# Attention scores, AV and a feed-forward layer on one core: AV fills its third PSUM tile last, and the exponentials of the second half are read in another order

## The chip, the cores and the metric

The kernel runs on one core of a Trainium2 chip. The core has a matmul engine (TensorE, "PE" in the profile; its weight loads stand as "PEld"), three engines for elementwise work (VectorE "DVE", ScalarE "ACT", GpSimd "POOL"), SyncE ("SP"), which here only issues transfers, and transfers between memory and the chip (DMA). The engines run side by side, each through its own queue in order, and wait for one another by semaphores. PE writes its results to PSUM; only ACT and DVE read them from there. The metric is the device time of one execution in microseconds; a kernel's time is the median of several executions.

## The reference

Inputs are q, k and v of shape (8, 8, 576, 64) (batch, heads, positions, head size) and two weight matrices of 512 x 2048 and 2048 x 512, all float32. Two attentions are added, and a feed-forward layer follows:

```python
q_d = q.reshape(B, H, Sd, 4, D).mean(axis=3)      # also k_d, v_d; Sd = 144
out_up = np.repeat(sm_attn(q_d, k_d, v_d), 4, axis=2)
mask = np.abs(pos[:, None] - pos[None, :]) < 4    # each position sees 7
out_local = softmax(where(mask, q @ k.T / sqrt(D), -1e9)) @ v
x = (out_up + out_local) as (4608 tokens, 512)
h = x @ w_in
out = (h / (1 + exp(-1.702 * h))) @ w_out
```

"Down" below is the attention over the 144 pooled positions, "local" the banded one over all 576.

## The kernel before

The feed-forward layer runs in nine groups of 512 tokens (`n_groups`, L1056). For each group `mm1` (L869) multiplies by w_in: 16 blocks of 128 hidden features, four matmuls of 512 columns each (L854), read out by ACT with the activation function (L865). Then `mm2` (L893) multiplies by w_out: 64 matmuls (L930) into two PSUM tiles PM in turn, read out by ACT (L915) and stored by SP.

The attention of batch b = g + 1 runs inside group g. The order of all engines is written out by hand (L43 to L45); there is no planner. `attention` (L804) gives five steps, and the list `POS` (L959) says before which matmul block each is issued: positions below 16 count the blocks of `mm1`, the others the matmuls of `mm2`. For batches 2 to 7 the steps are:

- position 12: scores of the first half (heads 0 to 3) on PE (`scores_mixed`, L402);
- position 16: their exponentials on ACT (`s_act`, L815), then the masks on DVE (`mask_local`, L459);
- position 33, that is before matmul 17 of `mm2`: scores of the second half (heads 4 to 7), and their exponentials and masks;
- position 41, before matmul 25, eight matmuls later: `avx` (L691) of heads 0 to 3, the weighted sums ("AV");
- position 53, before matmul 37, twelve matmuls later: `avx` of heads 4 to 7.

Batches 0 and 1 go by other functions.

Three PSUM tiles PA[0], PA[1], PA[2], of two banks each, serve the attention. The scores of a half lie in all three: down scores in PA[0], local scores in PA[1] and PA[2]. `exp_down` (L453) reads PA[0] into `ed`; `exp_local` (L446) reads PA[1] and then PA[2] into two `es` tiles (L448), in the loop `for u in range(2)`. In the second half `exp_down` comes first, so that ACT reads PA[0], PA[1], PA[2]. `mask_local` multiplies the two `es` tiles by the band mask in the order of their numbers.

`avx` then writes its sums over the same tiles. Its matmuls are short (57 to 144 columns) and use a quarter of the array each, so that four run side by side. `down` (L697) puts the pooled attention of one pair of heads into PA[0] and of the other into PA[2], numerators and denominators in turn, six calls of four matmuls (L701). `local` (L709, its matmul at L723) has three uses: `main` and `extra` with the calls beside them go to PA[0] and PA[2] (40 matmuls), `rest` and `rest_den` to PA[1] (24 matmuls). The order before is written at L744 to L760: `rest` and `rest_den` lie between the calls of `down`, and the main part follows.

What follows reads the tiles out (L765 to L772): ACT takes logarithms of the denominators in PA[0], PA[2] and PA[1], DVE copies the numerators in the same order (L767, L771), and ACT's exponential of the negated logarithms (L772) gives the reciprocals. DVE multiplies (L777), the pooled part is added (L793) by POOL for heads 0 to 3 and by DVE for heads 4 to 7, and xT is ready for `mm1`.

For the next batch DVE transposes q and k (`prep_1`, L284), and POOL sums them over four positions (`pool_qk`, L315 and L319), casts v (L325) and sums v into `vd` (`prep_v4`, L332 and L335). `down` needs `vd`.

Of the kernel before, what the change touches and what calls it, by code (L numbers as in the profile page):

```python
# [19 lines left out]
def kernel(  # L20
# [359 lines left out]
    def scores(b, qd, barred=False, sp=None):  # L380
        sp = sp or [ps_tile(), ps_tile()]
        if barred:
            bar_others(sp)
        for i in range(5):
            for a in range(2):
                for par in range(2):
                    for r in range(4):
                        rows = slice(32 * r, 32 * r + 32)
                        k0 = 114 * i + KSTART[par]
                        q0 = 114 * i + QSTART[par]  # L390
                        nc.tensor.matmul(  # L391
                            sp[r // 2][64 * par : 64 * par + 64, r % 2, 60 * i : 60 * i + 60],
                            lhsT=kT[b, qd][rows, k0 : k0 + 64, a],
                            rhs=qT[b, qd][rows, q0 : q0 + 60, a],
                            start=(a == 0 and not barred),
                            stop=(a == 1 or barred),
                            tile_position=(32 * r, 64 * par),
                            skip_group_check=barred,
                        )
        return sp  # L400

    def scores_mixed(b, qd, P):  # L402
        def local(i, a, half):
            for r in range(4):
                par = half if r < 2 else 1 - half
                rows = slice(32 * r, 32 * r + 32)
                k0 = 114 * i + KSTART[par]
                q0 = 114 * i + QSTART[par]
                nc.tensor.matmul(  # L409
                    P[1 + r // 2][64 * par : 64 * par + 64, r % 2, 60 * i : 60 * i + 60],  # L410
                    lhsT=kT[b, qd][rows, k0 : k0 + 64, a],
                    rhs=qT[b, qd][rows, q0 : q0 + 60, a],
                    start=(a == 0), stop=(a == 1),
                    tile_position=(32 * r, 64 * par),
                )

        if qd:
            for n in range(10):
                local(n // 2, n % 2, 0)
        for n in range(6):  # L420
            scores_d(b, qd, P[0], (n,))
            for a in range(2 if n < 5 else 0):
                local(n, a, 1)
        if not qd:
            for n in range(10):
                local(n // 2, n % 2, 0)
        return P[0], P[1:3]

    def scores_d(b, qd, sd=None, rounds=range(6)):
        sd = sd or ps_tile()  # L430
        bank = banks(sd)
        for n in rounds:
            kc, a = n // 2, n % 2
            for r in range(4):
                rows = slice(32 * r, 32 * r + 32)
                u, j = (r // 2, r % 2) if b < 2 else (r % 2, r // 2)
                nc.tensor.matmul(  # L437
                    bank[u][64 * j : 64 * j + 64, SD * kc : SD * kc + SD],
                    lhsT=kdT[qd][rows, 48 * kc : 48 * kc + 64, a],
                    rhs=qdT[b, qd][rows, :, a],  # L440
                    start=(a == 0), stop=(a == 1),
                    tile_position=(32 * r, 64 * j),
                )
        return sd

    def exp_local(qd, sp):  # L446
        for u in range(2):
            nc.scalar.activation(  # L448
                out=es[2 * qd + u][:, :, 0:300], in_=sp[u][:, :, 0:300],
                func=AF.Exp, scale=inv_sqrt_d,  # L450
            )
# [12 lines left out]
    def av(b, hp, n=None):  # L464
        o = ps_tile(n)
        av_local(b, hp, o)
        av_down(b, hp, o)
        return o
# [222 lines left out]
    def avx(b, hps):  # L691
# [5 lines left out]
        def down(kc, den):  # L697
            for u, hp in enumerate(hps):
                rows = slice(64 * u, 64 * u + 48)
                for j in range(2):  # L700
                    nc.tensor.matmul(  # L701
                        mains(u)[64 * j : 64 * j + 64, den, DN : DN + SD],
                        lhsT=ones[rows, 1, :] if den else vd[rows, kc, hp // 2 * 2 + j, 0:D],
                        rhs=eds[hp // 2][rows, j, SD * kc : SD * kc + SD],
                        start=(kc == 0), stop=(kc == 2),
                        tile_position=(64 * u, 64 * j),
                    )

        def local(den, to, what):  # L709
            for par in range(2):  # L710
                hp = hps[par] if to == "main" else hps[1 - par]
                i, c0, ni, n = what[par]
                rows = slice(64 * par, 64 * par + 64)
                if to == "rest":
                    t, bk = PA[1], par
                    at = 256 * den + 57 * (i - 1 + par)
                else:
                    t, bk = mains(par), den
                    at = 57 * i + c0 if par == 0 else 57 * i
                    if to == "extra":  # L720
                        at = EX
                for j in range(2):
                    nc.tensor.matmul(  # L723
                        t[64 * j : 64 * j + 64, bk, at : at + ni * n],
                        lhsT=ones[rows, 0, :] if den else vb[rows, i, 2 * hp + j, 0:D],
                        rhs=sub(es[hp][rows, j, :], 60 * i + c0, (60, ni), (1, n)),
                        start=True, stop=True,
                        tile_position=(64 * par, 64 * j),
                    )

        def rest(k):
            local(0, "rest", ((k + 1, 3, 1, 57), (k, 0, 1, 57)))

        def rest_den(k):
            local(1, "rest", ((k + 1, 3, 2, 57), (k, 0, 2, 57)))

        def main(k):
            local(0, "main", ((k, 3 if k else 0, 1, 57 if k else 60),
                              (k, 0, 1, 57 if k < 4 else 60)))

        def extra(den):
            local(den, "extra", ((0, 0, 1, 60), (4, 0, 1, 60)))

        for kc in range(3):  # L744
            down(kc, 0)
            rest(kc)
            down(kc, 1)
            if kc < 2:
                rest_den(2 * kc)
        rest(3)  # L750
        main(0)
        local(1, "main", ((1, 3, 2, 57), (0, 0, 2, 57)))
        main(1)
# [4 lines left out]
        extra(0)  # L758
        main(4)
        extra(1)  # L760

        l = work.tile([128, 2, S + SD], FP32, name="l", tag="l", bufs=2)
        n = work.tile([128, 2, S + SD], FP32, name="n", tag="n", bufs=1)
# [40 lines left out]
    def attention(b, slots=None):  # L804
        st = {}
        exps = "exp_and_others" if b == 1 else "natural_log_exp_and_others"

        def s_pe(qd):
            if b > 1:
                st["d", qd], st["s", qd] = scores_mixed(b, qd, PA)  # L810
                return
            st["d", qd] = scores_d(b, qd, PB[0])
            st["s", qd] = scores(b, qd, sp=PB[1:3])

        def s_act(qd):  # L815
            if qd == 0:
                nc.scalar.preload_act_table_set(exps)
            if b == 1 or qd:
                exp_down(qd, st["d", qd])
            exp_local(qd, st["s", qd])  # L820
            if b > 1 and not qd:
                exp_down(qd, st["d", qd])
            if qd == 1 and b == 1:
                nc.scalar.preload_act_table_set("silu_and_others")
            mask_local(qd)

        def s1():
            s_pe(1)
            s_act(1)

        def avn(*hps):
            def f():
                for hp in hps:
                    st["o", hp] = av(b, hp, slots and slots[hp % 2])
                for hp in hps:
                    st["y", hp] = normalise(st["o", hp])
            return f

        def tr(*hps):
            def f():  # L840
                for hp in hps:
                    st["x", hp] = transp(st["y", hp], slots and slots[hp % 2])
                for hp in hps:
                    od = copy_od(st["x", hp])
                    merge(b, hp, st["x", hp], od)
            return f

        first = [lambda: s_pe(0), lambda: s_act(0), s1]
        if b == 1:
            return first + [avn(0, 1), tr(0), tr(1), avn(2, 3), tr(2), tr(3)]  # L850
        return first + [lambda: avx(b, (0, 1)), lambda: avx(b, (2, 3))]
# [141 lines left out]
    sp = scores(0, 0, barred=True, sp=PA[0:2])  # L993
# [9 lines left out]
    sp = scores(0, 1, barred=True, sp=PA[0:2])  # L1003
# [52 lines left out]
    for g in range(n_groups):  # L1056
        b = g + 1
# [69 lines left out]
```

## Time and profile before

| what | value |
|---|---|
| median of 3 runs | 320.76 us (320.55 to 321.66) |
| profiled execution | 320.15 us |
| its span | 318.4 us |
| granted TensorE clock | 1.00 |
| PE busy | 305.3 us, 96% of the span |
| ACT, POOL, DVE busy | 200.1, 158.0, 141.9 us |
| one steady group (128.05 to 160.89 us) | 32.84 us, PE busy 32.75, ACT 23.58, POOL 20.76, DVE 17.54 |

A row of the timeline gives start, length, engine, line, operation, output and inputs with the tile's shape, and the number of instructions merged; a bracket says how long the engine stood idle before and whose end let it go on. The chain that ended last is followed back from the last instruction, at each step to what released it; its rows give start, length, and the engine and line. Matmuls are pipelined: one that begins while its predecessor is under way adds to the busy time, so the distance between two starts says more about PE than the length of a row.

### The profile page before, as it was taken

The numbers are of one execution on the slowest core, as the hardware profiler recorded it, in microseconds if no ns is written. First come the engines' busy times: TensorE is split into PE (matmuls) and PEld (weight loads), VectorE is DVE, ScalarE is ACT, GpSimd is POOL, SyncE is SP. The second block draws the span as 40 slices with busy tenths as digits, with TensorE's granted clock in tenths as the row PEclk, the third lists the DMA queues.
The fourth block names the chain that finished last, engine by engine and source line by source line (L and its number), as shares of the span: only waits on it lengthen the run. The fifth ranks groups of instructions, "written<-read, shape, count | busy, mean of one in ns | idle before, by whom it ended". The sixth has DMA issues, their size and how long they took to land.

```text
span 318.4 us, 10134 instructions
## 1 busy us (share of the span) xinstructions
PE 305.3 (96%) x4434; PEld 153.8 (48%) x4434; DVE 141.9 (45%) x283; ACT 200.1 (63%) x321; POOL 158.0 (50%) x183
## 2 busy tenths in 40 slices
PE   6688999999999999999999999999999999999995
PEld 2454454445554455445545454555445544444444
DVE  6983425820597049803890379127922580000000
ACT  4474782566786678557955885687568757315611
POOL 8883960198336963497339833992398020000000
PEclk9999999999999999999999999999999999999999
DMA  6999999999616980599149924993330110020011
GB/s 119 121 190 210 186 128 209 200 227 220 142 64 171 199 167 36 162 203 197 41 143 191 180 88 128 187 191 95 115 104 1 69 71 0 18 81 35 0 66 66
DMA packets 64124, 39.98 MB, mean 126 GB/s; under 512 B 44624, under 2 KB 54992, under 8 KB 64080
## 3 DMA queue, kind: packets, MB, share of 16 engines
q0 software_dynamic: 18864, 14.95, 33.1%
q1 hardware_dynamic: 45072, 24.32, 30.1%
q8 instruction: 34, 0.56, 0.8%
q14 instruction: 10, 0.08, 0.1%
q10 hardware_dynamic: 144, 0.07, 0.1%
HBM read 44.83 MB, written 9.44 MB: 170 GB/s over the span
## 4 chain that ended last, share of the span: by engine, by line
PE 88%; ACT 6%; DMA 4%; issue 1%; POOL 1%; DVE 0%; POOLq 0%
PE pm L930 33%; PE pm L854 26%; PE pa L854 14%; PE pa L409 3%; PE pa L930 2%; DMA qb<-in_q_dram 2%; PE pa L437 2%; PE pa L701 2%; ACT es L448 2%; PE pa L723 2%; ACT ed L454 2%; DMA vb<-in_v_dram 1%; PE pm L945 1%; PE pa L391 0%; ACT L1018 0%
## 5 line engine op out<-in xcount | busy, mean ns | idle before, releaser
L930 PE MATMUL pm<-w_out_bf,gT 128*128 128x512 bf16 x528 | 119.6, 379 | 0.0
L854 PE MATMUL pm<-xT,w_in_bf 128*128 128x512 bf16 x376 | 93.9, 379 | 0.7 <-ACT gT L865 0.5
L854 PEld LDWEIGHTS <-w_in_bf 128*128 128x128 bf16 x576 | 55.7, 98 | 67.1 <-issue 1.3
L865 ACT ACTIVATE gT<-pm 128x512 bf16<-128x512 f32 x94 | 56.2, 602 | 43.6 <-PE pm L854 43.6
L930 PEld LDWEIGHTS <-gT 128*128 128x128 bf16 x560 | 52.6, 98 | 61.1 <-issue 0.2
L462 DVE TENSOR_TENSOR es<-es,mask 128x600 bf16<-128x600 bf16 x28 | 18.8, 685 | 90.2 <-ACT es L448 89.4
L854 PE MATMUL pa<-xT,w_in_bf 128*128 128x512 bf16 x200 | 53.3, 379 | 0.0
L915 ACT ACTIVATE osb<-pm 128x512 f32<-128x512 f32 (+2 forms) x35 | 20.4, 582 | 32.8 <-PE pm L930 30.1
L793 POOL TENSOR_TENSOR xT<-xT,od 128x576 bf16<-128x576 bf16 x12 | 17.7, 1471 | 41.8 <-DVE xT L777 41.3
L315 POOL TENSOR_TENSOR pq<-kT 128x576 f32<-128x576 bf16 x14 | 16.2, 1157 | 37.9 <-DVE kT L284 37.8
L865 ACT ACTIVATE gT<-pa 128x512 bf16<-128x512 f32 x50 | 29.0, 607 | 5.6 <-PE pa L854 5.6
L777 DVE TENSOR_TENSOR xT<-n,l 128x285 bf16<-128x285 f32 (+1 forms) x96 | 28.2, 368 | 0.0
L332 POOL TENSOR_TENSOR pq<-v 112x512 f32<-112x512 f32 x18 | 24.0, 1331 | 0.8 <-DMA v<-in_v_dram 0.8
L917 DVE TENSOR_SCALAR osb<-pm 128x128 f32<-128x128 f32 x1 | 0.3, 293 | 53.5 <-ACT osb L915 53.5
L448 ACT ACTIVATE es<-pa 128x600 bf16<-128x600 f32 x32 | 19.7, 669 | 1.8 <-PE pa L391 1.7
L284 DVE STREAM_TRANSPOSE kT<-kb 128x576 f32<-128x576 f32 x16 | 19.9, 1247 | 1.8 <-DMA kb<-in_k_dram 1.8
L284 DVE STREAM_TRANSPOSE qT<-qb 128x576 f32<-128x576 f32 x16 | 19.9, 1242 | 0.2 <-DMA qb<-in_q_dram 0.2
L767 DVE COPY n<-pa 128x492 f32<-128x492 f32 x24 | 15.0, 665 | 9.2 <-ACT l L766 8.2
L766 ACT ACTIVATE l<-pa 128x492 f32<-128x492 f32 x24 | 12.6, 578 | 9.9 <-PE pa L723 9.9
L454 ACT ACTIVATE ed<-pa 128x864 bf16<-128x864 f32 x16 | 14.3, 894 | 5.3 <-PE pa L437 5.3
L772 ACT ACTIVATE l<-l 128x1440 f32<-128x1440 f32 x12 | 16.8, 1404 | 0.4
L237 POOL DMA_DIRECT2D vb<-in_v_dram x20 | 13.7, 700 | 5.9 <-DMA w_in_bf<-in_moe_w_in_dram 3.4
(120 smaller groups left out, 356.8 us busy)
## 6 DMA issues: line engine op xcount, KB each, us to landing
out_dram<-osb SPq DMA_DIRECT2D x34, 256.0 KB, 2.1
vf<-in_v_dram SPq DMA_DIRECT2D x60, 128.0 KB, 5.0
v<-in_v_dram SPq DMA_DIRECT2D x72, 96.0 KB, 3.3
kb<-in_k_dram POOLq DMA_DIRECT2D x16, 288.0 KB, 6.7
qb<-in_q_dram POOLq DMA_DIRECT2D x16, 288.0 KB, 8.9
w_out_bf<-in_moe_w_out_dram POOLq DMA_DIRECT2D x4, 512.0 KB, 13.3
vb<-in_v_dram POOLq DMA_DIRECT2D x20, 64.0 KB, 5.7
w_in_bf<-in_moe_w_in_dram POOLq DMA_DIRECT2D x2, 512.0 KB, 7.6
```

Source lines behind the costliest of these rows:

```text
L284: nc.vector.transpose(out=t32.rearrange("p (i c) -> p c i", c=18), in_=store[b, qd].bitcast(FP32).rearrange("p (c d) -> p c d", c=18),)
L332: eng.tensor_tensor(out=t1[0:112], in0=x[:, :, 0:2, :], in1=x[:, :, 2:4, :], op=ALU.add)
L448: nc.scalar.activation(out=es[2 * qd + u][:, :, 0:300], in_=sp[u][:, :, 0:300], func=AF.Exp, scale=inv_sqrt_d,)
L454: nc.scalar.activation(out=eds[qd][:, :, 0:432], in_=sd[:, :, 0:432], func=AF.Exp, scale=inv_sqrt_d / 16.0,)
L462: nc.vector.tensor_tensor(out=ev, in0=ev, in1=mask, op=ALU.mult)
L772: nc.scalar.activation(out=l, in_=l, func=AF.Exp, scale=-1.0)
L777: nc.vector.tensor_tensor(out=out, in0=sub(n, *part), in1=sub(l, *part), op=ALU.mult)
L793: eng.tensor_tensor(out=xs, in0=xs, in1=sub(od[:, u, :], 0, (1, SD), (0, 4)), op=ALU.add)
L854: nc.tensor.matmul(acc, lhsT=w_in_bf[:, dmc, ffc * 128 : (ffc + 1) * 128], rhs=xT[dmc][:, g * TG : g * TG + TG], start=(dmc == 0), stop=(d ...
L865: nc.scalar.activation(out=gT[:, ffc, :], in_=acc, func=AF.Silu, scale=GELU_SCALE)
L915: eng.activation(out=osb, in_=ap, func=AF.Copy, scale=1.0 / GELU_SCALE)
L930: nc.tensor.matmul(ops[t], lhsT=gT[:, ffc, t * 128 : (t + 1) * 128], rhs=w_out_bf[:, ffc, :], start=(ffc == 0), stop=(ffc == n_ffc - 1),)
```

## The change

In `avx` the calls that fill PA[1] move behind all others: the loop keeps the six `down` calls, and `rest` and `rest_den` come after `extra(1)`, in an order of their own. `exp_local` gets a parameter for the order of its two reads, and for batches from 2 on the second half (`qd` = 1) reads PA[2] before PA[1]. What is computed stays the same, and so do the number and the shapes of all instructions. `avx` runs twice in each of the batches 2 to 7; the exponentials' new order holds for the second half of each of them.

```diff
-    def exp_local(qd, sp):
-        for u in range(2):
+    def exp_local(qd, sp, us=(0, 1)):
+        for u in us:
             nc.scalar.activation(
                 out=es[2 * qd + u][:, :, 0:300], in_=sp[u][:, :, 0:300],
                 func=AF.Exp, scale=inv_sqrt_d,
...
         for kc in range(3):
             down(kc, 0)
-            rest(kc)
             down(kc, 1)
-            if kc < 2:
-                rest_den(2 * kc)
-        rest(3)
         main(0)
         local(1, "main", ((1, 3, 2, 57), (0, 0, 2, 57)))
         main(1)
...
         extra(0)
         main(4)
         extra(1)
+        for k in range(4):
+            rest(k)
+            if k % 2 == 0:
+                rest_den(k)
...
-            exp_local(qd, st["s", qd])
+            exp_local(qd, st["s", qd], (0, 1) if b == 1 or not qd else (1, 0))
```

## The prediction

> **What bounds the kernel now.** I read the page first: engine shares and the chain that ended last. The span is 318.4 us, the profiled execution 320.15 us.
>
> ```profile
> PE 305.3 (96%) x4434; PEld 153.8 (48%) x4434; DVE 141.9 (45%) x283; ACT 200.1 (63%) x321; POOL 158.0 (50%) x183
> ...
> PE 88%; ACT 6%; DMA 4%; issue 1%; POOL 1%; DVE 0%; POOLq 0%
> ```
>
> TensorE (PE) is the bound, yet 6% of the chain lies on ACT. A busy share can't show why: a short matmul counts some 0.2 us as busy and overlaps its successors, so it covers small gaps. So I took the chain in order of time for one steady batch, batch 4.
>
> ```profile
> 147.91 0.02 issue
> 147.93 0.89 ACT ed L454
> 148.82 1.13 ACT es L448 x2
> 149.95 0.04 issue
> 150.00 0.22 PE pa L701
> ```
>
> The second half's scores end at 147.91; the chain then leaves PE for the three exponentials of the half and returns 2.09 us later, at AV's "down" matmuls (L701). Between these, PE issued only eight matmuls of the second projection: 8 x 0.216 = 1.73 us. The remaining 0.36 us is a stall, met at the last of the three exponentials. The PE timeline of batch 3 names it.
>
> ```profile
> 114.87 1.90 PE L930 MATMUL pm<-w_out_bf,gT 128*128 128x512 bf16 x8
> 116.70 0.25 PE L701 MATMUL pa<-ed,vd 48*64 48x144 bf16 x2
> 117.16 0.25 PE L701 MATMUL pa<-ed,vd 48*64 48x144 bf16 x2 [0.20 <-ACT es L448]
> ...
> 118.25 2.76 PE L930 MATMUL pm<-w_out_bf,gT 128*128 128x512 bf16 x12
> 120.94 0.26 PE L701 MATMUL pa<-ed,vd 48*64 48x144 bf16 x4
> ...
> 122.05 3.20 PE L930 MATMUL pm<-w_out_bf,gT 128*128 128x512 bf16 x14
> ```
>
> Two "down" matmuls, into PA[0], run at 116.70. The next two write PA[2] and stand until 117.16, because PA[2] is read by the last exponential. AV of heads 0 to 3 takes 118.25 - 116.70 = 1.55 us; the same 88 matmuls for heads 4 to 7, with no stall, take 122.05 - 120.94 = 1.11. The difference is what PE loses. From the same rows of all six batches (2 to 7) it is 0.33, 0.44, 0.33, 0.33, 0.34, 0.33 us: 2.10 us together.
>
> **The exponentials swapped.** The reads of PA[1] and PA[2] have one shape, a mean of 669 ns on the page, so ACT's total stays. Its rows of batch 4:
>
> ```profile
> 147.93 0.89 ACT L454 ACTIVATE ed<-pa 128x864 bf16<-128x864 f32 x1 [0.47 <-PE pa L437]
> 148.72 1.23 ACT L448 ACTIVATE es<-pa 128x600 bf16<-128x600 f32 x2
> 151.19 1.05 ACT L766 ACTIVATE l<-pa 128x492 f32<-128x492 f32 x2 [1.25 <-PE pa L723]
> ```
>
> PA[2]'s becomes the first of the pair: ready at 148.72 + 0.67 = 149.39, and with the 0.04 us that the chain shows from ACT to PE, 149.43. AV starts at 149.66, so the wait is 0.23 us early; in batch 3 (115.88 + 0.67 + 0.04 = 116.59 against 116.70) 0.11, in batch 2 0.23. No remainder of the stall: -2.10 us on PE. PA[1]'s becomes the last, ready at 149.99.
>
> **The third tile filled last.** 24 of the 88 matmuls move behind the other 64. From the undisturbed AV of batch 4 (starts 154.09, 154.12 for a group of four with 57 columns; 154.19, 154.24 with 114) they take 4 x 0.03 + 2 x 0.055 = 0.23 us, the rest 1.10 - 0.23 = 0.87. So the first of them meets PA[1] at 149.66 + 0.87 = 150.53, 0.54 us after its exponential. This wait moves to PE's queue behind 64 matmuls and costs nothing; if it did stand, only the second projection's matmuls would be behind it. No step that issues a DMA moves, and neither POOL's nor SP's queue is passed.
>
> Whether these 24 cost more in a row than laid between 144-column ones no row shows. PE's timeline of the same AV has the nearest:
>
> ```profile
> 154.09 0.20 PE L723 MATMUL pa<-es,vb 64*64 64x57 bf16 x4
> 154.12 0.23 PE L701 MATMUL pa<-ed,ones 48*64 48x144 bf16 x4
> ...
> 154.66 0.26 PE L723 MATMUL pa<-es,vb 64*64 64x57 bf16 x12
> 154.76 0.20 PE L723 MATMUL pa<-es,ones 64*64 64x60 bf16 x4
> ```
>
> Twelve short ones in a row take 0.10 us from start to the next start, 8 ns each, against 0.23 / 24 = 10 ns as the 24 lie now. I take no change. Farther rows: batch 1's AV with 65 columns spends 0.28 us on 20 at L479, 14 ns each, which would add 24 x 0.014 - 0.23 = 0.11 us in each of 12 AVs, 1.3 us; and its slowest stretch, ten in 0.29 us at L501, 29 ns each, would add 0.47 x 12 = 5.6. Below nothing: if the six "down" groups (0.065 us for 144 columns each) and the short ones kept 8 ns per short matmul, 0.04 x 12 = 0.5 us less.
>
> **The waits behind.** DVE's two masks now both follow the last exponential, since DVE asks for es[2] first: they run from 149.99 at 0.47 us each (the pair's shortest) to 150.94. The copies out of PSUM queue behind them. A copy starts when ACT's logarithm of its tile is done (batch 3: 118.35 + 0.58 = 118.93, copy at 118.96). The logarithm of PA[0] needs only the first 64 matmuls, so it can start at 149.66 + 0.87 + 0.10 = 150.63 and end at 151.21: the masks are 0.27 us early. If they took the 1.91 us that the pair takes when POOL works beside it, the third copy would end near 153.8; the next AV writes PA[0] at 153.45, when its copy (152.55) is done, PA[2] likewise (153.2), and PA[1] only at 154.3. So hidden too.
>
> POOL is the close one. It sums v into vd without a pause until just before AV:
>
> ```profile
> 148.78 0.73 POOL L335 TENSOR_TENSOR vd<-pq 112x256 bf16<-112x256 f32 x1
> ```
>
> ready at 149.51, 0.15 us before AV. This POOL work starts where DVE ends its transposes (131.21), and DVE has worked without a pause since ACT's exponential of the logarithms at 121.29: 28.2 us from there. That exponential ended 4.46 us after AV's start in batch 4; by the start above it is 0.97 + 1.53 + 1.40 = 3.90. So vd comes earlier by 0.56 us against the previous AV's start, while the period shrinks by 0.33: the margin grows to about 0.38. Later than AV nothing on PE waits: mm1 and mm2 run through to the next scores, and after batch 7 to the end, so what PE saves reaches the end.
>
> **Sum.** 320.15 - 2.10 + 0 = 318.05 us for the profiled execution; the median of the runs, 320.76, lies 0.61 above that execution, so I forecast 320.76 - 2.10 = 318.7.
>
> **The rivals.**
> *Slower: short matmuls without cover.* Today each of the six groups starts behind four 144-column matmuls, whose 0.065 us can hide its issue and weight loads. Alone, each might pay its own. The gain is gone at 2.10 / 12 = 0.175 us more per AV, i.e. at (0.23 + 0.175) / 24 = 17 ns per matmul. At L501's 29 ns it is 320.76 - 2.1 + 5.6 = 324.3; at 14 ns, 319.9. For it: 57 columns are so short that anything fixed shows. Against it: the twelve in a row at 8 ns.
> The Trainium skill ("TensorE: Matmul & The Clock Gate", Back-to-back issue gap) gives matmuls of 1 to 64 columns a floor of about 25 ns each. By that floor 24 in a row would take 0.60 us and the time, as an estimate from that page, would be 323.1; the 8 ns in this trace lie far under it, so with four tiles of the array side by side the floor doesn't hold per matmul here.
> *POOL takes the wait's place.* If POOL's sums kept their times, AV of batch 6 could start no earlier than its vd is ready (214.45 + 0.73 = 215.18, for today's 215.32): 0.14 us for all batches up to there, and then the stalls of batches 6 and 7 alone (batch 7's vd is ready 2.6 us early): 0.14 + 0.34 + 0.33 = 0.81 us, 319.95. For it: a margin of 0.15 us. Against it: its chain starts from the work that comes earlier.
> *The wait stays.* If AV's first matmul into PA[2] waited for both exponentials, nothing changes: 320.8. Against it: today the two matmuls into PA[0] already run while the later exponentials are under way, so waits go by tile.
> *More.* 0.5 us from denser short matmuls: 318.2.
>
> **How the numbers follow.** Forecast 0.72; more 0.06; short matmuls at 14 ns 0.05, at 29 ns 0.05; POOL 0.06; wait stays 0.06. About 0.3% (1 us) is what a measurement of this kernel tells from no change. Faster by more: 0.72 + 0.06 = 0.78. Within: 0.05 + 0.06 + 0.06 = 0.17. Slower: 0.05. The range takes the forecast, "more" with the runs' scatter below it, and the 14 ns and POOL cases: 317.9 to 320.0.
>
> **What would show it.** AV of heads 0 to 3 lasts 1.10 us, as that of heads 4 to 7; the steady period falls from 32.84 to 32.50 us. In the chain the steady batches no longer pass through L454 and L448. ACT's first logarithm starts before the last L723 matmul ends. The masks start 0.6 us later after the scores and nobody waits for them. Wrong if: both AVs grow (short matmuls), L701 waits for POOL's vd, or L701 still waits for es.

## The result, and the profile after

The changed kernel takes 319.05 us (median of 20 runs, 317.75 to 322.25) against 321.35 for the kernel before, measured beside it (20 runs, 319.80 to 322.81). The ratio is 0.9936, 95% interval 0.9914 to 0.9958: 2.06 us less, 1.35 to 2.76. The prediction had 2.10 us less. One profile below, that of swap_only, comes from a slow run (325.35 us) that the ratios leave out; what it has over the others lies ahead of the stretch that is compared.

The profile's own numbers need care. These are lines of the changed kernel's page: the engine shares, the granted clock in 40 slices of the span, and the chain's shares by engine.

```profile
span 318.2 us, 10095 instructions
...
PEclk9977999999999999999999999999999999999999
...
PE 91%; POOL 3%; issue 3%; DMA 2%; DVE 0%; ACT 0%; POOLq 0%
```

ACT has gone from the chain (6% before, 0% now), but the span, 318.2 us, is that of before, 318.4. The third and fourth slice, 16 to 32 us, ran at a granted clock of 0.79, where the profiled execution of before had 1.00. That stretch lies ahead of all that the change touches. The clock alone does not set the length of this part: after_again, below, was granted 0.66 and 0.91 in the same two slices and reached the second AV of batch 2 at 88.3 us. So the spans are cut at a common point, the start of the second AV of batch 2: before, 88.0 us up to it and 230.4 from it; after, 89.9 and 228.3. The stretch that holds the first AVs of batches 3 to 7 is 2.0 us shorter (2.04 before rounding); the head, the part up to the cut, is longer by about as much, which is why the span shows nothing.

The chain in order of time for batch 4 (start, length, engine and line), first profile of the changed kernel:

```profile
149.21 0.08 PE pa L437 x4
149.29 0.16 issue
149.45 1.67 PE pm L930 x7
151.12 0.50 PE pa L701 x24
151.62 0.58 PE pa L723 x61
152.21 0.16 issue
152.37 2.54 PE pm L930 x11
```

It stays on PE from the scores through the second projection and AV. The two pieces "issue" are the places of a projection matmul whose record is missing (7 of 8 and 11 of 12 are there). A second profile of the changed kernel, that of after_again, has all records. Its PE timeline, batch 4:

```profile
148.93 0.59 PE L930 MATMUL pm<-w_out_bf,gT 128*128 128x512 bf16 x2
149.45 0.26 PE L701 MATMUL pa<-ed,vd 48*64 48x144 bf16 x4
149.54 0.23 PE L701 MATMUL pa<-ed,ones 48*64 48x144 bf16 x4
...
150.17 0.20 PE L723 MATMUL pa<-es,ones 64*64 64x60 bf16 x4
150.21 0.20 PE L723 MATMUL pa<-es,vb 64*64 64x57 bf16 x4
...
150.54 0.82 PE L930 MATMUL pm<-w_out_bf,gT 128*128 128x512 bf16 x3
```

The first four "down" matmuls run without a pause between the second and the third, and AV lasts 150.54 - 149.45 = 1.09 us, where batch 4 took 1.43 before; AV of heads 4 to 7 takes the same 1.09 (153.23 to 154.32). ACT, DVE and POOL of the same batch and profile:

```profile
147.72 0.89 ACT L454 ACTIVATE ed<-pa 128x864 bf16<-128x864 f32 x1 [0.47 <-PE pa L437]
148.51 1.23 ACT L448 ACTIVATE es<-pa 128x600 bf16<-128x600 f32 x2
150.42 1.05 ACT L766 ACTIVATE l<-pa 128x492 f32<-128x492 f32 x2 [0.68 <-PE pa L723]
```

```profile
149.77 0.85 DVE L462 TENSOR_TENSOR es<-es,mask 128x600 bf16<-128x600 bf16 x2 [2.59 <-ACT es L448]
151.04 1.25 DVE L767 COPY n<-pa 128x492 f32<-128x492 f32 x2 [0.41 <-ACT l L766]
```

```profile
148.39 0.73 POOL L335 TENSOR_TENSOR vd<-pq 112x256 bf16<-112x256 f32 x1
```

The exponentials still end 0.29 us after AV's start (148.51 + 1.23 = 149.74), yet PE no longer stands for the second of them. The first logarithm starts 0.97 us after AV's start instead of 1.53 and before AV's last matmuls are over. The masks end at 150.62, 0.4 us ahead of the copies, and vd is complete at 149.12, 0.33 us ahead of AV.

### The profile page after: what moved, and what is told of

It reads as the page before. It is cut to its first block, busy times and chain, and to the rows that moved or that the text cites. A ratio compares the mean times of both kernels' runs of the same rounds, so it can differ in the third digit from the quotient of the medians.

```text
span 318.2 us, 10095 instructions
## 1 busy us (share of the span) xinstructions
PE 302.2 (95%) x4389; PEld 154.1 (48%) x4434; DVE 139.8 (44%) x283; ACT 200.4 (63%) x321; POOL 155.9 (49%) x183
## 4 chain that ended last, share of the span: by engine, by line
PE 91%; POOL 3%; issue 3%; DMA 2%; DVE 0%; ACT 0%; POOLq 0%
PE pm L930 35%; PE pm L854 25%; PE pa L854 14%; PE pa L409 3%; PE pa L930 2%; PE pa L723 2%; PE pa L437 2%; PE pa L701 2%; DMA vb<-in_v_dram 2%; POOL vb L237 1%; PE pm L945 1%; PE pa L616 1%; PE pa L558 0%; PE pa L391 0%; POOL kb L206 0%
## 5 line engine op out<-in xcount | busy, mean ns | idle before, releaser
L930 PE MATMUL pm<-w_out_bf,gT 128*128 128x512 bf16 x503 | 114.7, 379 | 3.3 <-issue 3.0
L854 PE MATMUL pm<-xT,w_in_bf 128*128 128x512 bf16 x361 | 92.7, 381 | 0.9 <-ACT gT L865 0.5
L462 DVE TENSOR_TENSOR es<-es,mask 128x600 bf16<-128x600 bf16 x28 | 17.0, 643 | 98.5 <-ACT es L448 98.3
L793 POOL TENSOR_TENSOR xT<-xT,od 128x576 bf16<-128x576 bf16 x12 | 15.8, 1319 | 42.1 <-DVE xT L777 42.0
L454 ACT ACTIVATE ed<-pa 128x864 bf16<-128x864 f32 x16 | 14.3, 894 | 5.8 <-PE pa L437 5.8
```

The costliest lines, as they stand in the source:

```text
L462: nc.vector.tensor_tensor(out=ev, in0=ev, in1=mask, op=ALU.mult)
L854: nc.tensor.matmul(acc, lhsT=w_in_bf[:, dmc, ffc * 128 : (ffc + 1) * 128], rhs=xT[dmc][:, g * TG : g * TG + TG], start=(dmc == 0), stop=(d ...
L930: nc.tensor.matmul(ops[t], lhsT=gT[:, ffc, t * 128 : (t + 1) * 128], rhs=w_out_bf[:, ffc, :], start=(ffc == 0), stop=(ffc == n_ffc - 1),)
```

## The experiments

Since the head, the part up to the second AV of batch 2, varies from run to run, each kernel is given by its ratio to the kernel before, by the stretch from the second AV of batch 2 to the end (five first AVs lie in it), and by the distance from the start of a first AV to that of the second one in the same batch, where PE's stall shows.

| kernel | ratio (95% interval) | stretch, us | first to second AV, us |
|---|---|---|---|
| before | 1 | 230.4 | 4.13 to 4.24 |
| changed kernel | 0.9936 (0.9914 to 0.9958) | 228.3 | 3.78 |
| after_again | 0.9911 (0.9879 to 0.9943) | 228.3 | 3.78 |
| swap_only | 0.9995 (0.9969 to 1.0020) | 230.3 | 4.07 to 4.24 |
| order_only | 0.9990 (0.9966 to 1.0014) | 230.1 | 4.11 to 4.12 |
| later_av | 0.9946 (0.9921 to 0.9971) | 229.6 | 3.80 to 3.89 |
| early_av | 0.9956 (0.9935 to 0.9977) | 229.9 | 4.42 to 4.56, two more matmuls between |
| before_half | 1.0085 (1.0064 to 1.0106) | 233.0 | 4.58 to 4.74 |
| after_half | 0.9940 (0.9918 to 0.9962) | 229.2 | 3.84 to 3.99 |
| after_pool | 0.9930 (0.9909 to 0.9952) | 229.1 | 3.78 to 3.98 |

Where the last column has a range of 0.09 us or more, ACT began 0.11 to 0.17 us later after the scores in some batches than in the others (see the last section); in after_pool the reason is another, given there. In the kernel before this is batch 3 alone, with 4.24. Inserted lines move line numbers in three of the kernels: L707 and L729 in the two with half an exponential more, L702 in after_pool, stand for L701 and L723, and L454 in before_half is the repeated exponential.

**after_again: the changed kernel once more.** No edit.

> The changed kernel once more, beside the partial ones. Theory (the stall at AV's first matmuls into PA[2] is gone, and nothing takes its place): 2.1 us less than before, ratio 0.9935; the steady batches repeat at 32.46 us instead of 32.83, AV of heads 0 to 3 as long as AV of heads 4 to 7 (1.08 us). Rival (the gain seen was the runs' scatter): ratio 1.000.

Its interval overlaps that of the first comparison, and the stretch is the same to 0.1 us. The steady batches come every 32.47 us (32.83 before). The gain repeats.

**swap_only: the exponentials alone.**

```diff
-    def exp_local(qd, sp):
-        for u in range(2):
+    def exp_local(qd, sp, us=(0, 1)):
+        for u in us:
...
-            exp_local(qd, st["s", qd])
+            exp_local(qd, st["s", qd], (0, 1) if b == 1 or not qd else (1, 0))
```

> Only the exponentials are swapped; AV keeps its order, in which the fifth matmul writes PA[1]. Theory (AV waits tile by tile, so now the wait is for PA[1], whose exponential is last): the stall stays but for the two matmuls into PA[2] that now run before it, 0.03 to 0.06 us; 0.0 to 0.4 us less than before, ratio 0.999 to 1.000, and the wait stands at L723 instead of L701. Rival (the swap alone frees PE, AV's order is for nothing): 2.1 us less, ratio 0.9935.

No difference to before, as the theory had it: the interval allows at most 1.0 us less, not the rival's 2.1. PE's timeline of batch 5 shows where the wait went. The list of waits (from 95 to 255 us; us in total, times, longest) names its releaser in the one batch, the fourth, where it passes 0.2 us:

```profile
187.25 0.59 PE L930 MATMUL pm<-w_out_bf,gT 128*128 128x512 bf16 x2
187.78 0.26 PE L701 MATMUL pa<-ed,vd 48*64 48x144 bf16 x4
188.12 0.22 PE L723 MATMUL pa<-es,vb 64*64 64x57 bf16 x4
```

```profile
PE pa L723 <- ACT es L448: 0.2, 1, 0.2
```

Now four matmuls run, and the fifth, the first into PA[1], stands for the last exponential. AV is 1.38 us long instead of 1.44 (1.54 in batch 4).

**order_only: AV's order alone.** The exponentials read PA[1] before PA[2], as before.

```diff
-            exp_local(qd, st["s", qd], (0, 1) if b == 1 or not qd else (1, 0))
+            exp_local(qd, st["s", qd])
```

> Only AV's order is changed; ACT reads PA[1] before PA[2]. Theory (the third and fourth matmul write PA[2], whose exponential is last again): AV of heads 0 to 3 keeps 0.3 us of stall at L701; 0.0 to 0.4 us less than before (AV is 0.02 us shorter in 12 places), ratio 0.999 to 1.000. Rival (the order itself is the gain, by denser matmuls or by logarithms that start earlier): 2 us less, ratio 0.994.

Again as the theory had it, with at most 1.1 us less by the interval. In PE's timeline of batch 4 the first group of four stretches over the wait, from 150.06 to 150.41, where it takes 0.09 us undisturbed:

```profile
150.06 0.59 PE L701 MATMUL pa<-ed,vd 48*64 48x144 bf16 x4
150.41 0.31 PE L701 MATMUL pa<-ed,ones 48*64 48x144 bf16 x4
```

The logarithms do start earlier here (1.29 us after AV's start instead of 1.53), and it buys nothing that can be told from noise. The stretch is 0.3 us shorter: 0.11 of this is batch 3, where ACT began later in the profile of before, and AV itself is nearly 0.02 us shorter at each of ten places. So neither part works without the other: each leaves one of the two tiles that AV wants early behind the last exponential.

**later_av: the wait covered by other work.** The kernel before, both AVs two projection matmuls later.

```diff
-    POS = [12, 16, 33, 41, 53]
+    POS = [12, 16, 33, 43, 55]
```

> The kernel before, with both AVs two matmuls of the second projection later (0.43 us), so that these cover the exponentials; order and exponentials as before. Theory (all of the gain is PE's wait for the last exponential, 0.33 to 0.44 us a batch): the wait is gone here too, 1.9 to 2.1 us less than before, ratio 0.994. Rival (the gain comes from PA[0] and PA[2] being read out earlier, while PE still fills PA[1]): nothing of that changes here, ratio 1.000.

Faster than before, by 1.7 us of 321.36 (0.9 to 2.5), so covering the wait gains most of what the change's two parts gain. The profile shows 0.8 us in the stretch and 0.3 more in batch 2. From first to second AV, 4.13 fell to 3.80 in batches 2, 3 and 7, the expected third of a microsecond, and to 3.84 to 3.89 in batches 4 to 6, where ACT began later and 0.04 to 0.09 us of the stall stayed; and 0.14 to 0.22 came back between the second AV and the next first one. PE's timeline at the start of the next `mm1`, and DVE's:

```profile
129.02 0.59 PE L854 MATMUL pa<-xT,w_in_bf 128*128 128x512 bf16 x2
129.60 0.38 PE L854 MATMUL pm<-xT,w_in_bf 128*128 128x512 bf16 x1
```

```profile
128.80 1.42 DVE L793 TENSOR_TENSOR xT<-xT,od 128x576 bf16<-128x576 bf16 x2
```

The two matmuls from 129.02 are done issuing at 129.45; the next stands until 129.60. It is the first that reads xT of heads 4 and 5, and DVE's addition for these heads, the first of the pair from 128.80, is over by about half of 1.42 us, near 129.5. An AV that is issued later hands xT over later: here a new wait takes part of the old one's gain. In the changed kernel the same two matmuls start at 128.98 and the next one at 129.41, with no wait.

**early_av: less cover.** The changed kernel, its first AV two projection matmuls earlier.

```diff
-    POS = [12, 16, 33, 41, 53]
+    POS = [12, 16, 33, 39, 53]
```

> The changed kernel, with AV of heads 0 to 3 two matmuls of the second projection earlier (0.43 us less cover). Theory (the exponential of PA[2] is ready only 0.07 to 0.08 us before AV in batches 2 to 6 and 0.2 in batch 7, by the trace of the changed kernel): a stall of 0.35 us in five batches and 0.2 in one comes back, 1.9 us more than the changed kernel, so about 0.2 us less than before, ratio 0.999. Rival (with the new order AV no longer depends on the exponentials' time): as the changed kernel, 0.9935.

In the trace the stall is back by the expected amount: 4.55 us from first to second AV, less the two matmuls (0.43) and the 3.78 of the changed kernel, is 0.34 us in batches 3 to 6, and 0.21 in batches 2 and 7. Batch 4 on PE and ACT:

```profile
148.42 0.59 PE L701 MATMUL pa<-ed,vd 48*64 48x144 bf16 x4
148.77 0.31 PE L701 MATMUL pa<-ed,ones 48*64 48x144 bf16 x4
```

```profile
148.05 1.23 ACT L448 ACTIVATE es<-pa 128x600 bf16<-128x600 f32 x2
```

The first exponential ends near 148.05 + 0.67 = 148.72, and the group that waited for it goes on. The stretch, 229.9 us, is 1.6 longer than the changed kernel's. The timed runs do not confirm the expected total: 0.9956 is 1.4 us under the kernel before (0.7 to 2.1), so the expected 0.999 lies outside the interval and the rival's 0.9935 at its edge. The traces give some 0.6 us under the kernel before, just below the interval: 0.4 to 0.5 in the stretch and 0.14 in batch 2. It is the trace that decides for the theory here, since the stall stands in it row by row. Why the timed runs are better is not known. One candidate, not tested, is that the one profile of the kernel before is a good one: ACT began late in one of its six batches, which cost it 0.11 us, and in before_half, with the same order of AV and exponentials, in four.

**before_half and after_half: the same extra work on ACT, in both kernels.** Half of the last exponential of the second half is done twice.

```diff
+    def exp_again(qd, sp, u):
+        nc.scalar.activation(
+            out=es[2 * qd + u][:, 0, 0:300], in_=sp[u][:, 0, 0:300],
+            func=AF.Exp, scale=inv_sqrt_d,
+        )
...
+            if b > 1 and qd:
+                exp_again(qd, st["s", qd], 1)   # 0 in after_half
```

> The kernel before, with half of the last exponential of the second half (PA[2], 300 elements) done a second time: by the distances of the rows (0.56 us for 600 elements, 0.79 for 864) some 0.31 us more on ACT ahead of AV in each of six batches. Theory (AV stands at the last exponential): all of it is seen, 6 x 0.31 = 1.9 us more than before, ratio 1.006. Rival (the stall at AV is something else): ratio 1.000.

> The changed kernel, with half of its last exponential (PA[1], 300 elements) done a second time: 0.31 us more on ACT ahead of the third tile's matmuls. Theory (AV meets PA[1] 0.76 us after its start, and this exponential is then ready at 0.44 + 0.31 + 0.04 = 0.79): nearly all of it is hidden, 0 to 0.3 us more than the changed kernel, ratio to before 0.9935 to 0.9945. Rival (AV waits for all exponentials together, and the change shortened something else): 1.9 us more, ratio 0.9995.

The dose was larger than expected. ACT and PE of before_half, batch 5:

```profile
183.95 1.23 ACT L448 ACTIVATE es<-pa 128x600 bf16<-128x600 f32 x2
185.21 0.42 ACT L454 ACTIVATE es<-pa 128x300 bf16<-128x300 f32 x1
```

```profile
184.75 0.25 PE L707 MATMUL pa<-ed,vd 48*64 48x144 bf16 x2
185.68 0.25 PE L707 MATMUL pa<-ed,vd 48*64 48x144 bf16 x2 [0.69 <-ACT es L454]
```

The repeat starts only when the exponential before it is over (185.18), so it adds 185.63 - 185.18 = 0.45 us and not 0.31. PE stands from the second matmul until 185.68: the whole dose is seen. From first to second AV it is 0.45 us in batches 4 and 7 and 0.49 in batch 3, where ACT began at about the same time as in the profile of before, and 0.59 to 0.61 in the others, where it began later; 2.6 us over five batches in the stretch, 2.7 us in the timed runs (2.1 to 3.4), which hold all six. In the changed kernel the same dose costs 0.07 us in batches 2, 5 and 7 and 0.20 in 3, 4 and 6, 0.8 in all where 0 to 0.3 was expected of the smaller dose, and the wait has moved to the third tile. The stretch is 0.9 us longer; 0.1 of it lies between two batches and is not explained. The timed ratio, 0.9940, is within what was expected and too coarse to tell these sizes apart. PE's timeline of after_half, batch 3:

```profile
117.72 0.20 PE L729 MATMUL pa<-es,ones 64*64 64x60 bf16 x4
117.95 0.22 PE L729 MATMUL pa<-es,vb 64*64 64x57 bf16 x4
```

Between the last group into PA[0] and PA[2] and the first into PA[1] lie 0.23 us where 0.03 is undisturbed. So the changed kernel has 0.25 us of room for the last exponential where ACT begins late and nearly 0.4 where it begins early (the dose of 0.45 less what is seen of it), and the kernel before had none.

**after_pool: more work on POOL.** One sum of q, 128x288, is done twice ahead of the sums of v.

```diff
-            nc.gpsimd.tensor_tensor(
-                out=dst, in0=t1[:, :, 0, :], in1=t1[:, :, 1, :], op=ALU.add
-            )
+            for _ in range(2 if b > 1 and qd and name == "q" else 1):
+                nc.gpsimd.tensor_tensor(
+                    out=dst, in0=t1[:, :, 0, :], in1=t1[:, :, 1, :], op=ALU.add
+                )
```

> The changed kernel, with one sum on POOL (128x288, 0.67 us) done a second time ahead of the sums of v. Theory (vd is ready 0.37 us before AV in batches 3 to 6, and POOL's chain starts from the preceding AV): AV waits for vd 0.30 us in these four batches, 1.2 us more than the changed kernel, ratio to before 0.997, with the wait at L701 for L335. Rival (POOL has room, or catches up, since it stands idle for over 11 us in each batch): no change, ratio 0.9935.

Half of the expected 1.2 us came. From first to second AV the loss is 0.17 to 0.20 us in batches 3 to 5 and 0.05 in batch 6, 0.6 us together; the stretch is 0.8 longer, and the timed ratio is too coarse to show it (the expected 0.997 lies outside its interval). vd is ready 0.37 us before AV's start in the changed kernel and 0.37 to 0.39 us after it here (0.25 in batch 6), so POOL's chain moved by the whole dose and AV did not wait for it at its start. POOL and PE, batch 5:

```profile
182.27 0.73 POOL L336 TENSOR_TENSOR vd<-pq 112x256 bf16<-112x256 f32 x1
```

```profile
182.62 0.26 PE L702 MATMUL pa<-ed,vd 48*64 48x144 bf16 x4
...
182.83 0.23 PE L702 MATMUL pa<-ed,ones 48*64 48x144 bf16 x4
183.05 0.26 PE L702 MATMUL pa<-ed,vd 48*64 48x144 bf16 x4
```

Four groups run while POOL still writes the last third of vd (until 183.00). Only the fifth group, which reads that third, stands, from 182.89 to 183.05, 0.16 us. AV needs the last part of vd 0.27 us after its start, and this is room that the working of the prediction left out.

## Why the prediction was right, point by point

**The stall and its cause.** Confirmed. The two matmuls at 116.70 and the pair at 117.16 were read as a wait for PA[2] alone. swap_only and order_only show the wait at the tile whose exponential is last, at the second or at the first group of AV; before_half shows that it grows with that exponential; later_av removes all or most of it without either part of the change.

**The size.** 2.10 us from six differences of AV lengths. The trace gives 0.46 us from first to second AV in batch 3 and 0.35 in the others, 2.2 together; the timed runs 2.06 (1.35 to 2.76), so the agreement of the medians to 0.04 us is closer than the runs can tell, and in part luck. The 0.02 us by which each batch exceeds its stall is AV's own length, 1.09 us instead of 1.10 to 1.11.

**The short matmuls in a row.** "No change" was right to 0.02 us. The row at 150.21 begins the 24; the next projection matmul is at 150.54, 0.33 us later with the 0.10 to 0.13 us in which any AV hands over to the projection, so 0.20 to 0.23 us for the 24, as when they lay between longer ones. The rival that asks 14 or 29 ns for each falls. Its two rows had been misread: the ten matmuls at L501 have a row of 0.29 us, but that counts the last one's own 0.19, so their starts lie within 0.10; and twenty at L479 take 0.18 us from their first start (49.17) to that of the next row (49.35), not 0.28. Both are 9 to 11 ns each, so neither of the rival's prices stands in a row of before. What falls too is the floor of about 25 ns that the Trainium skill gives for matmuls of up to 64 columns ("TensorE: Matmul & The Clock Gate", Back-to-back issue gap), as far as it is read per matmul: here it is 8 to 10 ns, with four tiles of the array side by side (sixteen of the 24 have 57 columns; the other eight, with 114, the prediction's estimate by the page counted among the short ones).

**The exponential of PA[2] ready in time.** Right, with less room than written in places. 0.23 us was expected in batch 4, and the second profile has it there (148.51 + 0.67 + 0.04 = 149.22 for 149.45). In batches 3, 5 and 6 of that profile, and in batches 2 to 6 of the first, it is only 0.06 to 0.10 us, because ACT starts 0.13 to 0.17 us later after the scores; the prediction had this case in batch 3 (0.11). By these figures one projection matmul (0.22 us) less ahead of AV would already cost something in those batches.

**The waits behind.** They hid, as forecast, with other sizes. The 24 begin 150.21 - 149.45 = 0.76 us after AV's start and not 0.87: the working took their 0.23 us from AV's whole length, which also holds the 0.10 us of the handover. So the room for PA[1]'s exponential is 0.47 us in batch 4 and 0.30 where ACT begins late, instead of 0.54, and less by the 0.04 us from ACT to PE. The logarithm came at 0.97 us as forecast, but by luck: instead of 0.87 + 0.10 it is 0.72 for the start of the last group into PA[0] and PA[2] (150.17), 0.20 for that group, and 0.05 until ACT starts. vd was ready 0.33 to 0.37 us ahead of AV, forecast 0.38. The masks end 0.4 us ahead of the copies, forecast 0.27.

**POOL as a rival.** Its chance was small and it did not come, but its margin was wrong. The step that failed is the point of need: the working set the readiness of all of vd against AV's first matmul, and after_pool shows that AV needs the last third 0.27 us later. The margin was nearly 0.6 us, not 0.38: vd moved by 0.74 to 0.76 us and AV lost 0.16 to 0.20.

**The absolute time.** 318.7 was worked out from a median of 320.76; the twenty runs of the result have 321.35 for the kernel before and 319.05 for the changed one. The difference held; both levels lie higher by 0.35 to 0.6 us, and no run here says why.

## What to carry to other kernels

When an engine frees several tiles one after the other and another engine refills them, write down the two orders side by side: the refill should take the tiles in the order in which they come free, and, as here, changing one of the two orders alone may gain nothing. Read such a stall from distances between starts of equal pieces of work, and not from the length of rows, since short pipelined matmuls cover it in the busy share (PE reads 96% busy before, and after 97% in the profile that has all records, 95% in the one that lacks some). When a margin is judged, set each part of an operand against the first instruction that reads that part.

## What was not expected of the hardware

ACT's start after the last matmul of the scores has two values. Over the profiles of all kernels with AV at its old place, the exponential of the down scores starts either 1.72 to 1.73 or 1.55 to 1.61 us before AV; the idle time before it is 0.46 to 0.48 us in most of the former rows and 0.59 to 0.64 in most of the latter. Both occur within one execution, with the same instructions; the cause is open. It decides here between 0.2 and less than 0.1 us of room.

The head up to the second AV of batch 2, in which only one first AV lies, took 87.4 to 93.3 us over these profiles. In four of the ten the granted clock was below 1.00 between 16 and 32 us (0.79 over these 16 us in three of them, 0.89 in later_av), in the others 1.00; swap_only, with the longest head, also had 0.79 from 48 to 56 us. The clock does not order the heads: 88.3 us in after_again with 0.79, 89.3 in before_half with 1.00. The stretch behind the head was the same to 0.1 us in the two profiles of the changed kernel, the only one profiled twice.
